# Strassen groups in a fused attention and MLP kernel: the first product of a group copied into the PSUM bank of the second

## The chip, the cores and the metric

The kernel runs on one NeuronCore of a Trainium2 chip. The metric is the device time of one execution in microseconds (us); less is better. Where several executions were timed, the median is given.

## The reference

Inputs are q, k and v of shape (8, 8, 576, 64): batch, heads, sequence, head dimension. A linear attention is followed by a layer norm and a two-layer MLP with a residual:

```python
q_s = softmax(q, axis=-1)             # over the 64 of the head
k_s = softmax(k, axis=2)              # over the sequence
kv  = einsum('bhsd,bhse->bhde', k_s, v)  # 64 x 64 for each head
x   = (q_s @ kv) as (8, 576, 512)     # heads side by side
xn  = (x - mean(x)) / sqrt(var(x) + 1e-6) * g_ln
out = x + relu(xn @ w_ch1) @ w_ch2    # 512 -> 2048 -> 512
```

All inputs and the output are float32; the kernel multiplies in 16 bit types. The first matrix product of the MLP, xn @ w_ch1 with its relu, is the part that the change touches.

## The kernel before

**Tiling.** The 8 x 576 tokens are cut into nine chunks of 512: chunks 0 to 7 hold the first 512 tokens of each batch entry (transposed tokens in `xsT`), and chunk 8 (`xT8`) holds the last 64 tokens of all eight. For each chunk the first MLP product gives `hT`, 16 row blocks of 128 hidden units by 512 tokens in float16, and the second (`mm2_split`, line 735) multiplies that with w_ch2. `attn(b + 1)` for the next batch entry (queries, keys, values, the products kv, xT and xT_last) runs beside the MLP of entry b.

**Order of the work.** No engine decides its order at run time. Each step is a task of the class `Plan` (line 100) with an engine, an assumed duration, what it reads and writes, and a class number. `Plan.order` plays the schedule through with these durations and an assumed 0.12 us from one engine to another; whenever an engine is free it takes the ready task with the lowest class. The instructions are then emitted in that order, and each engine works through its own list strictly. The table `SHIFT` (line 22) adds a number to the class of a task by its name and by the phase that it was made in: `early` for chunks 1 and 2, `steady` for 3 to 6, `last` for 7, `end` for 8. Tasks made for chunk 0, and the attention of batch entry 1, are made with no phase, and no entry of the table applies to them (line 137).

**The seven-product groups.** From chunk 3 on `mm1_seven` (line 882) makes the first MLP product. Most row blocks are made by `direct` (line 940): four matmuls of 128x512 into one of the four PSUM banks `pg`, and a relu on ScalarE (line 631). Some groups of four row blocks, the units n = 1 and n = 3, are made by a Strassen-Winograd scheme with seven products instead of eight. `UNITS` (line 841) says which: unit 1 in chunks 3 to 6, units 1 and 3 in chunks 7 and 8, eight units in all. A product is four matmuls of 128x256 (line 914). A unit holds three PSUM banks: `g[0]`, `g[1]` and `g[2]`, all three from the four banks `pa` that the attention products use too. It has three SBUF buffers `cp` for partial sums: the tiles `cp0` to `cp2`, which `add_x` and `final` of `mm2_split` use as well, or in chunks 7 and 8 the staging tiles `stg`.

The steps of a unit that the change and the prediction touch are:

- product "11" x "11" into bank `g[0]`, which stays open for further products
- `copy(0, 0)` (line 920): ScalarE copies this bank to the SBUF buffer 0
- product "12" x "21" into bank `g[1]`, as a group of its own
- `end(1, 0, 0, 0)` (lines 933 and 936): VectorE adds bank `g[1]` and buffer 0 into `hT`, then takes the maximum with 0 in place
- the rest: products "S2" x "T2" and "S3" x "T3" added to `g[0]`, two more copies (L920), further ends; a quarter of `hT` needs no partial sum and gets its relu on ScalarE directly (line 930)

**Other users of PSUM.** `mm2_split` takes three `pg` banks in turn for each chunk (gc, gb, ga, line 738) and holds ga from its first product to its last. Banks are given out in turn (`nxt`, line 297), in the order in which tasks are made, and not by which one is free.

**Loads.** SyncE's queue issues loads, transposes and stores. The loads of q, k and v land in `stg`, and ScalarE reads them from there: exponentials at lines 424 and 454, a cast at line 464.

Of the kernel before, what the change touches and what calls it, by code (L numbers as in the profile page):

```python
# [13 lines left out]
FP16 = mybir.dt.float16  # L14
BF16 = mybir.dt.bfloat16
U32 = mybir.dt.uint32
AF = mybir.ActivationFunctionType
# [2 lines left out]


SHIFT = {
    ('add_x1', 'early'): 0.6,
    ('add_x1', 'last'): -0.4,
    ('add_x1', 'steady'): 0.6,
    ('copy1', 'last'): 0.1,
    ('copy1', 'steady'): -0.1,
    ('direct1', 'last'): 1,
    ('dma_t1', 'early'): 0.2,
    ('dma_t1', 'steady'): -0.1,  # L30
    ('end1', 'end'): 0.4,
    ('end2', 'last'): -0.4,
    ('end2', 'steady'): 0.4,
    ('end3', 'end'): -0.6,
    ('end3', 'last'): -0.4,
    ('end3', 'steady'): 0.2,
    ('end4', 'end'): 0.1,
    ('final1', 'early'): -1,
    ('final1', 'end'): -0.1,
    ('final1', 'last'): 0.1,  # L40
    ('final2', 'end'): -0.6,
    ('final3', 'early'): 1,
    ('final3', 'end'): 1,
    ('final3', 'last'): 0.2,
    ('final3', 'steady'): 0.2,
    ('keys1', 'steady'): -0.4,
    ('kv1', 'early'): -0.4,
    ('kv1', 'steady'): -1,
    ('kv2', 'early'): 0.1,
    ('kv2', 'steady'): 0.6,  # L50
    ('kv3', 'early'): 0.4,
    ('kv4', 'early'): 0.1,
    ('load1', 'early'): 0.6,
    ('load1', 'steady'): -0.1,
    ('mm11', 'early'): -0.4,
    ('product1', 'end'): 0.1,
    ('product2', 'steady'): -1,
    ('queries1', 'early'): -0.4,
    ('queries1', 'steady'): -0.4,
    ('queries2', 'early'): -0.2,  # L60
    ('queries2', 'steady'): 0.2,
    ('queries3', 'early'): -1,
    ('queries3', 'steady'): -0.2,
    ('queries4', 'early'): -1,
    ('relu_evac1', 'early'): 0.4,
    ('relu_evac1', 'last'): 0.4,
    ('relu_evac1', 'steady'): -0.1,
    ('store2', 'early'): -0.1,
    ('store2', 'last'): 0.4,
    ('store2', 'steady'): 0.1,  # L70
    ('tokens3', 'early'): 0.2,
    ('tokens3', 'last'): 1,
    ('tokens6', 'last'): 0.1,
    ('tokens6', 'steady'): 0.6,
    ('tokens7', 'early'): 0.2,
    ('tokens7', 'last'): 0.4,
    ('tokens7', 'steady'): -0.6,
    ('tokens8', 'early'): -0.2,
    ('tokens8', 'last'): 0.2,
    ('tokens9', 'early'): -1,  # L80
    ('tokens9', 'steady'): 0.2,
    ('tt1', 'early'): 0.2,
    ('tt1', 'end'): -1,
    ('tt1', 'last'): 0.6,
    ('tt1', 'steady'): 1,
    ('tt3', 'early'): 1,
    ('tt3', 'steady'): -1,
    ('tt4', 'steady'): 0.6,
    ('values3', 'steady'): -0.1,
    ('xT1', 'early'): 1,  # L90
    ('xT1', 'steady'): -0.1,
    ('xT3', 'early'): -0.6,
    ('xT3', 'steady'): 0.2,
    ('xT_last1', 'steady'): 0.4,
    ('xT_last2', 'early'): 0.1,
    ('xT_last2', 'steady'): -0.4,
}


# [114 lines left out]
def act_t(n, extra=0.0):  # L214
    return 0.19 + 0.000833 * n + extra
# [7 lines left out]
def kernel(  # L223
# [10 lines left out]
    nc = tc.nc  # L234
    B, H, SEQ, D = q.shape
    DM = H * D
    DH = 4 * DM
    P = 128
# [14 lines left out]
    def sb(shape, dt, name):  # L253
        return persist.tile(shape, dt, name=name, tag=name)
# [42 lines left out]
    def nxt(what, n):  # L297
        i = cnt[what] % n
        cnt[what] += 1
        return i  # L300
# [23 lines left out]
    def sk(s):  # L324
        return [("stg", s, 0), ("stg", s, 1)]
# [268 lines left out]
    def tokens(c, cls=1, after=(), stats=()):  # L594

        x, xk, sti, stk = xof(c)
        if c < B:
            src, r = xsT[c % 2], XK(c % 2)
        else:
            src, r = xT8, [("xT8", b, i) for b in range(B) for i in range(2)]  # L600
        i = None
        for hf in range(2) if c == 0 else ():
            t = nxt("pa", 4)
            v = pa[t].bitcast(FP16)
            def f(hf=hf, v=v):
                for n in range(8):
                    nc.tensor.transpose(v[:, n * P : n * P + P], src[:, 8 * hf + n, :], ident_h)
            plan.task("tokens1", "PE", 0.52, f, r=r + ["ident_h"], w=[("pa", t)], cls=0, after=after)
            plan.task("tokens2", "DVE", dve_t(1024, 2), lambda hf=hf, v=v: nc.vector.tensor_copy(
                x[:, 2 * hf : 2 * hf + 2, :], v.rearrange("p (j n) -> p j n", j=2)), r=[("pa", t)], w=[(xk, 2 * hf), (xk, 2 * hf + 1)], cls=cls)  # L610
        if c:
            i = plan.task("tokens3", "SP", 2.2, lambda: nc.sync.dma_start_transpose(x.rearrange("p j (k c) -> p (j k) c", k=KO1), src.rearrange("p n t -> p (n t)")),
                     r=r, w=[(xk, j) for j in range(J)], mb=0.9, land=0.6, after=after)
        for j in STATS_ACT.get(c, ()):
            plan.task("tokens4", "ACT", act_t(512, 0.1), lambda j=j: nc.scalar.activation(junk, x[:, j, :], AF.Copy, saturate=False, scale=-(DM ** -1.5), accum_out=bmv[:, j, 0:1]),
                     r=[(xk, j)], w=[("bmv", j), "junk"], cls=SCLS, slack=2.0, after=stats)
            plan.task("tokens5", "ACT", act_t(512, 0.1), lambda j=j: nc.scalar.activation(junk, x[:, j, :], AF.Square, saturate=False, bias=bmv[:, j, 0:1], scale=DM ** -0.5, accum_out=bmv[:, j, 1:2]),
                     r=[(xk, j)], w=[("bmv", j), "junk"], cls=SCLS)
        for j in set(range(J)) - set(STATS_ACT.get(c, ())):
            plan.task("tokens6", "DVE", dve_t(512), lambda j=j: nc.vector.bn_stats(bst[:, j, :], x[:, j, :]), r=[(xk, j)], w=[("bst", j)], cls=cls, slack=2.0 if c else 0.0, after=stats)  # L620
            plan.task("tokens7", "DVE", 0.18, lambda j=j: nc.vector.bn_aggr(bmv[:, j, :], bst[:, j, :]), r=[("bst", j)], w=[("bmv", j)], cls=cls)
        plan.task("tokens8", "ACT", 0.3, lambda: nc.scalar.activation(sti[:, 3, :], bmv[:, :, 1], AF.Ln, bias=eps, scale=GS * GS),
                 r=["eps"] + [("bmv", j) for j in range(J)], w=[(stk, "v", j) for j in range(J)], cls=0)
        state["rstd"] = plan.task("tokens9", "ACT", 0.2, lambda: nc.scalar.activation(sti[:, 4, :], sti[:, 3, :], AF.Exp, scale=-0.5),
                                 r=[(stk, "v", j) for j in range(J)], w=[(stk, "r", j) for j in range(J)], cls=0)
        return i
# [215 lines left out]
    UNITS = {3: (1,), 4: (1,), 5: (1,), 6: (1,), 7: (1, 3), 8: (1, 3)}  # L842
    SUMS_AT = {2: (1,), 6: (3,)}
    flat = lambda t, n: t.bitcast(FP16).rearrange("p a j c -> p (a j c)")[:, :n].rearrange("p (i k n) -> p i k n", i=n // 512, k=2)
    WS = [flat(eq[n // 2], 1536) if n % 2 == 0 else sb([P, 3, 2, 256], FP16, f"WS{n}") for n in range(4)]
    WSK = [[("eq", n // 2, 0), ("eq", n // 2, 1)] if n % 2 == 0 else [] for n in range(4)]
    SLOT = (0, 1, None, 2)

    def w1_sums(n, before):
# [32 lines left out]
    def mm1_seven(c):  # L882
# [14 lines left out]
        class Unit:  # L897
            def __init__(self, n):
                self.n = n
                if last:  # L900
                    a = 3 * (n % 2)
                    self.g = [bufs[a + i] for i in range(3)] if n ^ 1 in units else [(pa[i], ("pa", i)) for i in [nxt("pa", 4) for _ in range(3)]]
                    self.cp = [(stg[a + i][:, :512], sk(a + i)) for i in range(3)]
                else:
                    self.g = [(pa[i], ("pa", i)) for i in [nxt("pa", 4) for _ in range(3)]]
                    self.cp = [(cp[i], [("cp", i)]) for i in range(3)]

            def product(self, a, b, g, first, last):
                fa, (fb, kb) = A[a], Bm[b]
                bank, bk = self.g[g]  # L910
                def f():
                    for i in range(2):
                        for k in range(2):
                            nc.tensor.matmul(bank[:, 256 * i : 256 * i + 256], fa(self.n, k, i), fb(k),  # L914
                                             start=(first and i == 0 and k == 0), stop=(last and k == 1), skip_group_check=True)
                ids.append(plan.task("product2", "PE", 0.437, f, r=kb + ([("WS", self.n, int(a[1]) - 1)] if a[0] == "S" else []), w=[bk]))

            def copy(self, g, n):
                bank, bk = self.g[g]
# [29 lines left out]
        for n0 in (0, 2):  # L949
            us = [Unit(n) for n in (n0, n0 + 1) if n in units]  # L950
            for u in us:
                u.product("11", "11", 0, True, False)
                u.copy(0, 0)
                u.product("12", "21", 1, True, True)
                u.end(1, 0, 0, 0)
            for u in us:
                u.product("S2", "T2", 0, False, False)
                u.copy(0, 1)
# [111 lines left out]
```

## Time and profile before

| what | value |
|---|---|
| median of six runs | 274.26 us (273.57 to 274.64) |
| the profiled execution's own time | 274.23 us |
| its span, first to last instruction | 272.4 us |
| PE busy | 264.0 us, 97% of the span |
| VectorE (DVE) busy | 228.1 us, 84% |
| ScalarE (ACT) busy | 170.0 us, 62% |
| granted TensorE clock | 0.998 |

The span is the time between the first and the last instruction in the trace; 1.83 us of the profiled execution's 274.23 us lie outside it. PE is TensorE. A matmul's row in the profile lasts longer than the time until the next one can start: a 128x256 matmul shows 273 ns, yet four of them in a row take 0.44 us. So PE busy is a union of overlapping rows, and progress on PE is read from the starts.

### The profile page before, as it was taken

The page shows a single profiled execution, that of the slowest core. Times are in us where ns is not written, and L with a number is a line of the kernel's source. Part 1 is how long each engine was busy: PE and PEld are TensorE (multiplying, and loading weights), DVE is VectorE, ACT ScalarE, POOL GpSimd, SP SyncE. Part 2 cuts the span into 40 slices and gives each one's busy share as a digit, 9 for nine tenths or more (in the row PEclk, how much of TensorE's full clock was granted, in tenths as well). Part 3 has the DMA queues.
Part 4 walks back from the last instruction along what each step waited for, and adds up shares of the span by engine and source line. Part 5 has one row for each costly group of instructions (what it writes and reads, how often), then busy time and mean ns, then how long its engine had stood idle before and what let it go on. Part 6 is the DMA issues. An engine that isn't in the chain of part 4 may idle for free.

```text
span 272.4 us, 5957 instructions
## 1 busy us (share of the span) xinstructions
PE 264.0 (97%) x2415; PEld 172.4 (63%) x2415; DVE 228.1 (84%) x484; ACT 170.0 (62%) x282; POOL 1.7 (1%) x12
## 2 busy tenths in 40 slices
PE   8799999999999999999999999999999999999994
PEld 3333445346864488548865786578558886786683
DVE  2897998898969889988998899989998897875772
ACT  4777866689598596578546955676562268325500
POOL 2000000000000000000000000000000000000000
PEclk9999999999999999999999999999999999999999
DMA  7999999699979999899288945995650960005004
GB/s 262 363 386 388 388 388 236 187 314 269 327 259 169 200 391 127 151 312 322 57 147 247 370 80 106 232 378 126 155 88 2 141 170 1 2 0 147 10 2 154
DMA packets 55875, 54.85 MB, mean 201 GB/s; under 512 B 34596, under 2 KB 35112, under 8 KB 55848
## 3 DMA queue, kind: packets, MB, share of 16 engines
q1 hardware_dynamic: 55696, 54.34, 71.7%
q8 instruction: 19, 0.31, 0.5%
q10 hardware_dynamic: 152, 0.13, 0.1%
q14 instruction: 8, 0.07, 0.1%
HBM read 36.70 MB, written 9.44 MB: 169 GB/s over the span
## 4 chain that ended last, share of the span: by engine, by line
PE 84%; DMA 9%; ACT 2%; SPq 1%; DVE 1%; issue 1%; ACTq 0%
PE pg L748 31%; PE pg L945 20%; PE pg L668 11%; PE pa L914 9%; DMA stg<-in_moe_w_ch_dram 7%; PE pg L812 5%; DMA stg<-in_k_dram 2%; PE pa L475 2%; PE pa L506 1%; PE pa L668 1%; PE pa L748 1%; SPq L321 1%; ACT ek L454 1%; PE pa L529 0%; PE pg L372 0%
## 5 line engine op out<-in xcount | busy, mean ns | idle before, releaser
L631 ACT ACTIVATE hT<-pg 128x512 f16<-128x512 f32 x102 | 60.2, 596 | 37.9 <-PE pg L945 28.4
L748 PEld LDWEIGHTS <-S 128*128 128x128 f16 x512 | 49.6, 98 | 7.1 <-DVE ot L759 0.4
L945 PE MATMUL pg<-xsT,w_sb 128*128 128x512 f16 x224 | 52.9, 379 | 0.0
L748 PE MATMUL pg<-T,S 128*128 128x256 f16 x368 | 43.6, 273 | 0.0
L748 PEld LDWEIGHTS <-hT 128*128 128x128 f16 x384 | 37.2, 98 | 7.4 <-issue 1.6
L945 PEld LDWEIGHTS <-w_sb 128*128 128x128 f16 x256 | 24.8, 98 | 23.2
L668 PE MATMUL pg<-xsT,w_sb 128*128 128x512 f16 x168 | 37.6, 379 | 0.7 <-DVE w_sb L378 0.7
L668 PEld LDWEIGHTS <-w_sb 128*128 128x128 f16 x184 | 17.4, 97 | 22.4 <-DVE w_sb L378 1.5
L684 DVE TENSOR_TENSOR S<-hT 128x1024 f16<-128x1024 f16 x32 | 21.6, 683 | 9.9 <-ACT hT L631 8.1
L748 PE MATMUL pg<-w_sb,hT 128*128 128x256 f16 x248 | 29.2, 273 | 0.0
L759 DVE SCALAR_TENSOR_TENSOR ot<-pg,st,cp 128x256 f32<-128x256 f32 x47 | 20.5, 477 | 6.6 <-PE pg L748 6.5
L426 DVE TENSOR_REDUCE zq<-eq 128x18 f32<-128x1152 bf16 x16 | 21.5, 1344 | 4.6 <-ACT eq L424 4.6
L759 DVE SCALAR_TENSOR_TENSOR cp<-pg,st,x 128x256 f32<-128x256 f32 x46 | 20.2, 478 | 5.8 <-PE pg L748 5.4
L620 DVE BATCH_NORM_STATS2 bst<-x 128x6 f32<-128x512 f16 x36 | 23.7, 675 | 0.0
L424 ACT ACTIVATE eq<-stg 128x1152 bf16<-128x1152 f32 x16 | 18.5, 1163 | 7.6 <-DMA stg<-in_q_dram 7.6
L430 DVE TENSOR_TENSOR eq<-eq,rzq 128x1152 bf16<-128x1152 bf16 x16 | 21.7, 1357 | 0.5
L519 ACT CAST xsT<-pa 128x512 f16<-128x512 f32 x31 | 16.0, 595 | 6.8 <-PE pa L506 6.8
L454 ACT ACTIVATE ek<-stg 128x1152 bf16<-128x1152 f32 x16 | 18.6, 1166 | 2.5 <-DMA stg<-in_k_dram 2.5
L464 ACT CAST vb<-stg 128x1152 f16<-128x1152 f32 x15 | 17.1, 1166 | 1.9 <-DMA stg<-in_v_dram 1.8
L748 PE MATMUL pg<-w_sb,S 128*128 128x256 f16 x128 | 15.6, 273 | 0.0
L914 PEld LDWEIGHTS <-w_sb 128*128 128x128 f16 x128 | 12.4, 98 | 4.7
L812 PE MATMUL pg<-w_sb,hT 128*128 128x512 f16 x64 | 14.7, 380 | 0.0
(100 smaller groups left out, 292.7 us busy)
## 6 DMA issues: line engine op xcount, KB each, us to landing
stg<-in_q_dram SPq DMA_DIRECT2D x16, 576.0 KB, 5.7
stg<-in_k_dram SPq DMA_DIRECT2D x16, 576.0 KB, 7.4
stg<-in_v_dram SPq DMA_DIRECT2D x16, 576.0 KB, 8.9
out_dram<-ot SPq DMA_DIRECT2D x33, 256.0 KB, 4.4
stg<-in_moe_w_ch_dram SPq DMA_DIRECT2D x16, 512.0 KB, 10.5
out_dram<-ot SPq DMA_DIRECT2D x1, 512.0 KB, 2.8
out_dram<-ot SPq DMA_DIRECT2D x1, 128.0 KB, 2.7
out_dram<-ot ACTq DMA_DIRECT2D x1, 128.0 KB, 2.2
```

What stands on the lines that cost most here:

```text
L426: plan.task("queries2", "DVE", dve_t(QW), lambda: nc.vector.reduce_sum(zq[:, hf], eh, axis=AX.X), r=[("eq", u, hf)], w=[("zq", hf)], cls=q ...
L430: plan.task("queries4", "DVE", dve_t(QW), lambda: nc.vector.tensor_tensor(eh, eh, rzq[:, hf].to_broadcast([P, 2 * JT, D]), op=ALU.mult), r ...
L454: plan.task("keys1", "ACT", act_t(QW), lambda: nc.scalar.activation(ek[u][:, hf].rearrange("p j (s d) -> p s j d", s=2), sv(s), AF.Exp), r ...
L620: plan.task("tokens6", "DVE", dve_t(512), lambda j=j: nc.vector.bn_stats(bst[:, j, :], x[:, j, :]), r=[(xk, j)], w=[("bst", j)], cls=cls, ...
L631: nc.scalar.activation(hT[:, m, :], bank, AF.Relu)
L668: nc.tensor.matmul(bank[gi], w1_sb[:, ko, m * P : m * P + P], xt[:, ko], start=(ko == 0), stop=(ko == KO1 - 1))
L684: plan.task("tt1", "DVE", dve_t(256 * n, 2), lambda: nc.vector.tensor_tensor(S[i][:, ks], a, b, op=op), r=r, w=sk(i), cls=(-0.25 if i < 2 ...
L748: nc.tensor.matmul(g[i][0], fa(k, i), fb(k), start=(first and k == 0 and (i == 0 or g[0][1] != g[1][1])), stop=(last and k == HK - 1), ski ...
L759: nc.vector.scalar_tensor_tensor(dst[:, i, :], in0=g[i][0], scalar=sti[:, 4, 2 * t0 + i : 2 * t0 + i + 1], in1=src[:, i, :], op0=ALU.mult, ...
L812: nc.tensor.matmul(pg[gis[j]], hT[:, kk, j * P : j * P + P], w2_sb[:, kk, :], start=(kk == 0), stop=(kk == KO2 - 1))
L914: nc.tensor.matmul(bank[:, 256 * i : 256 * i + 256], fa(self.n, k, i), fb(k), start=(first and i == 0 and k == 0), stop=(last and k == 1), ...
L945: nc.tensor.matmul(bank, w1_sb[:, ko, m * P : m * P + P], xt[:, ko], start=(ko == 0), stop=(ko == KO1 - 1))
```

## The change

Five things are edited.

1. A new method `seed` copies bank `g[0]` with ScalarE into bank `g[1]`, in place of the copy into SBUF. The product "12" x "21" is then made without a start flag, so that it adds to what the copy wrote. The end of this quarter becomes the ScalarE relu of line 930; the VectorE add and maximum are dropped for it.
2. Bank `g[1]` of every unit comes from `pg` and no longer from `pa`. The cases for chunks 7 and 8 are written as one rule with the others.
3. `WS[0]` and `WS[2]`, weight sums for the units 0 and 2, are placed in other tiles. `UNITS` has only units 1 and 3, so neither is written or read.
4. The assumed durations of `tokens4` and `tokens5` are changed. `STATS_ACT` is empty, so no such task is made.
5. The table `SHIFT` is replaced by another one with some 80 entries, among them three for `seed1`.

```diff
 SHIFT = {
-    ('kv2', 'early'): 0.1,
-    ('kv3', 'early'): 0.4,
-    ('load1', 'early'): 0.6,
+    ('keys1', 'early'): 1,
+    ('kv2', 'early'): -1,
+    ('kv3', 'early'): 0.2,
+    ('load1', 'early'): 0.2,
+    ('seed1', 'end'): 0.6,
+    ('seed1', 'last'): -1,
+    ('seed1', 'steady'): -0.1,
...
 class Unit:
     def __init__(self, n):
         self.n = n
-        if last:
-            a = 3 * (n % 2)
-            self.g = [bufs[a + i] for i in range(3)] if n ^ 1 in units else [(pa[i], ("pa", i)) for i in [nxt("pa", 4) for _ in range(3)]]
-            self.cp = [(stg[a + i][:, :512], sk(a + i)) for i in range(3)]
-        else:
-            self.g = [(pa[i], ("pa", i)) for i in [nxt("pa", 4) for _ in range(3)]]
-            self.cp = [(cp[i], [("cp", i)]) for i in range(3)]
+        new = lambda name, ts: (lambda i: (ts[i], (name, i)))(nxt(name, 4))
+        self.g = [new("pa", pa), new("pg", pg), new("pa", pa)]
+        a = 3 * (n % 2)
+        self.cp = [(stg[a + i][:, :512], sk(a + i)) if last else (cp[i], [("cp", i)]) for i in range(3)]
...
+    def seed(self, g, d):
+
+        (bank, bk), (to, tk_) = self.g[g], self.g[d]
+        plan.task("seed1", "ACT", act_t(512), lambda: nc.scalar.copy(to, bank), r=[bk], w=[tk_], cls=-0.3)
...
     for u in us:
         u.product("11", "11", 0, True, False)
-        u.copy(0, 0)
-        u.product("12", "21", 1, True, True)
-        u.end(1, 0, 0, 0)
+        u.seed(0, 1)
+        u.product("12", "21", 1, False, True)
+        u.end(1, 0, 0)
```

More of the change, by code (lines that the diff above doesn't have):

```diff
@@ L22 @@
 SHIFT = {
-    ('add_x1', 'early'): 0.6,
-    ('add_x1', 'last'): -0.4,
+    ('add_x1', 'early'): -0.1,
+    ('add_x1', 'end'): 0.1,
+    ('add_x1', 'last'): 1,
     ('add_x1', 'steady'): 0.6,
[L26 to L42, printed above, removed]
+    ('copy1', 'end'): 0.6,
+    ('copy1', 'last'): -0.1,
+    ('copy1', 'steady'): 0.1,
+    ('direct1', 'end'): -0.1,
+    ('direct1', 'last'): -1,
+    ('direct1', 'steady'): 0.1,
+    ('dma_t1', 'steady'): 0.1,
+    ('end1', 'end'): 0.2,
+    ('end1', 'last'): -0.2,
+    ('end1', 'steady'): 0.2,
+    ('end2', 'end'): 0.4,
@@ L43 @@
+    ('end2', 'last'): 0.6,
+    ('end2', 'steady'): 0.2,
+    ('end3', 'steady'): -0.2,
+    ('end4', 'end'): -0.1,
+    ('final1', 'early'): 0.6,
+    ('final1', 'end'): 0.4,
+    ('final1', 'last'): -0.2,
+    ('final2', 'end'): -0.2,
+    ('final3', 'early'): 0.4,
     ('final3', 'end'): 1,
-    ('final3', 'last'): 0.2,
+    ('final3', 'last'): -0.4,
     ('final3', 'steady'): 0.2,
-    ('keys1', 'steady'): -0.4,
+    ('final4', 'end'): -0.4,
+    ('keys1', 'early'): 1,
+    ('keys1', 'steady'): 0.1,
@@ L47 @@
     ('kv1', 'early'): -0.4,
-    ('kv1', 'steady'): -1,
-    ('kv2', 'early'): 0.1,
-    ('kv2', 'steady'): 0.6,
-    ('kv3', 'early'): 0.4,
-    ('kv4', 'early'): 0.1,
-    ('load1', 'early'): 0.6,
[L54 to L62, printed above, removed]
-    ('queries3', 'steady'): -0.2,
@@ L64 @@
[L64 to L73, printed above, removed]
-    ('tokens6', 'steady'): 0.6,
[L75 to L79, printed above, removed]
@@ L80 @@
-    ('tokens9', 'early'): -1,
-    ('tokens9', 'steady'): 0.2,
+    ('kv2', 'early'): -1,
+    ('kv2', 'steady'): 0.4,
+    ('kv3', 'early'): 0.2,
+    ('kv4', 'early'): -0.4,
+    ('kv4', 'steady'): 0.2,
+    ('load1', 'early'): 0.2,
+    ('mm11', 'early'): 0.4,
+    ('product1', 'end'): 0.4,
+    ('product1', 'last'): -0.6,
+    ('product1', 'steady'): -0.6,
+    ('product2', 'end'): -0.1,
+    ('product2', 'last'): -0.1,
+    ('queries1', 'steady'): 0.2,
+    ('queries2', 'early'): 1,
+    ('queries2', 'steady'): 0.1,
@@ new lines @@
+    ('queries3', 'early'): -0.6,
+    ('queries3', 'steady'): -0.2,
+    ('queries4', 'steady'): -0.6,
+    ('relu_evac1', 'early'): 0.1,
+    ('relu_evac1', 'end'): 0.6,
+    ('relu_evac1', 'steady'): -1,
+    ('seed1', 'end'): 0.6,
+    ('seed1', 'last'): -1,
+    ('seed1', 'steady'): -0.1,
+    ('store1', 'end'): 0.6,
+    ('store2', 'early'): 1,
+    ('store2', 'last'): -0.4,
+    ('store2', 'steady'): -1,
+    ('tokens3', 'early'): 0.1,
+    ('tokens3', 'last'): -0.1,
+    ('tokens3', 'steady'): -0.1,
@@ L82 @@
+    ('tokens6', 'early'): 0.1,
+    ('tokens6', 'last'): 1,
+    ('tokens6', 'steady'): 0.6,
+    ('tokens8', 'early'): -1,
+    ('tokens8', 'last'): -0.2,
+    ('tokens9', 'early'): 0.6,
+    ('tokens9', 'last'): 0.4,
+    ('tokens9', 'steady'): 1,
     ('tt1', 'early'): 0.2,
-    ('tt1', 'end'): -1,
-    ('tt1', 'last'): 0.6,
-    ('tt1', 'steady'): 1,
+    ('tt1', 'end'): 0.6,
+    ('tt1', 'last'): 0.4,
+    ('tt1', 'steady'): -0.4,
     ('tt3', 'early'): 1,
-    ('tt3', 'steady'): -1,
-    ('tt4', 'steady'): 0.6,
@@ L89 @@
[L89 to L96, printed above, removed]
+    ('tt3', 'steady'): -0.6,
+    ('tt4', 'last'): 0.1,
+    ('tt4', 'steady'): -0.1,
+    ('values3', 'steady'): 1,
+    ('xT1', 'early'): -0.2,
+    ('xT3', 'early'): 0.1,
+    ('xT_last2', 'early'): -0.4,
+    ('xT_last2', 'steady'): 0.4,
 }
@@ L614, in tokens @@
         for j in STATS_ACT.get(c, ()):
-            plan.task("tokens4", "ACT", act_t(512, 0.1), lambda j=j: nc.scalar.activation(junk, x[:, j, :], AF.Copy, saturate=False, scale=-(DM ** -1.5), accum_out=bmv[:, j, 0:1]),
+            plan.task("tokens4", "ACT", act_t(512, 0.23), lambda j=j: nc.scalar.activation(junk, x[:, j, :], AF.Copy, saturate=False, scale=-(DM ** -1.5), accum_out=bmv[:, j, 0:1]),
                      r=[(xk, j)], w=[("bmv", j), "junk"], cls=SCLS, slack=2.0, after=stats)
-            plan.task("tokens5", "ACT", act_t(512, 0.1), lambda j=j: nc.scalar.activation(junk, x[:, j, :], AF.Square, saturate=False, bias=bmv[:, j, 0:1], scale=DM ** -0.5, accum_out=bmv[:, j, 1:2]),
+            plan.task("tokens5", "ACT", act_t(512, 0.32), lambda j=j: nc.scalar.activation(junk, x[:, j, :], AF.Square, saturate=False, bias=bmv[:, j, 0:1], scale=DM ** -0.5, accum_out=bmv[:, j, 1:2]),
                      r=[(xk, j)], w=[("bmv", j), "junk"], cls=SCLS)
@@ L844 @@
     flat = lambda t, n: t.bitcast(FP16).rearrange("p a j c -> p (a j c)")[:, :n].rearrange("p (i k n) -> p i k n", i=n // 512, k=2)
-    WS = [flat(eq[n // 2], 1536) if n % 2 == 0 else sb([P, 3, 2, 256], FP16, f"WS{n}") for n in range(4)]
-    WSK = [[("eq", n // 2, 0), ("eq", n // 2, 1)] if n % 2 == 0 else [] for n in range(4)]
+    WS = [ek[0], None, eq[0], None]
+    WS = [sb([P, 3, 2, 256], FP16, f"WS{n}") if n % 2 else flat(WS[n], 1536) for n in range(4)]
+    WSK = [[("ek", 0, 0), ("ek", 0, 1)], [], [("eq", 0, 0), ("eq", 0, 1)], []]
     SLOT = (0, 1, None, 2)
```

## Prediction, made before the changed kernel was run

> **What bounds the kernel now.** I read the page's table of engines first:
>
> ```profile
> PE 264.0 (97%) x2415; PEld 172.4 (63%) x2415; DVE 228.1 (84%) x484; ACT 170.0 (62%) x282; POOL 1.7 (1%) x12
> ```
>
> PE is busy for 97% of the span. Since a matmul's row outlasts its share of PE, this alone proves little, so the second view is the busy time in stretches of 10 us (columns: PE, PEld, DVE, ACT, POOL, clock, DMA share, GB/s):
>
> ```profile
> 30.00:40.00 10.00, 10.00 (x48) 4.54 (x47) 9.51 (x14) 7.31 (x9) 0.00 (x0) 1.00 1.05 387
> ...
> 70.00:80.00 10.00, 9.57 (x155) 7.57 (x156) 7.02 (x20) 7.07 (x11) 0.00 (x0) 1.00 0.92 343
> ...
> 110.00:120.00 10.00, 10.00 (x122) 5.27 (x120) 9.33 (x25) 5.75 (x12) 0.00 (x0) 1.00 0.98 220
> ...
> 220.00:230.00 10.00, 10.00 (x79) 7.48 (x77) 8.02 (x19) 8.81 (x18) 0.00 (x0) 1.00 0.27 70
> ```
>
> From 30 to 260 us PE has 10.00 in every stretch except 70 to 80. The rates agree: the chain of work in order of time gives 3.49 us for 32 matmuls of 128x256 and 0.86 us for four of 128x512, 109 and 216 ns each, back to back. Third, PE's own waits and the end of the chain:
>
> ```profile
> PE pa L506 <- ACT kve L489: 0.4, 1, 0.4
> ```
>
> ```profile
> 27.63 7.08 PE pg L668 x32
> ...
> 267.66 0.89 PE pa L748 x8
> 268.55 0.03 issue
> 268.57 0.48 DVE ot L759
> ```
>
> The one wait of PE after 27.6 us is 0.43 us near 76.3 us, behind kve on ScalarE. So 27.6 us are a start limited by weight loads, 241 us are PE without gaps but for that one, and 3.8 us (272.4 - 268.6) are the last VectorE step and store. Nothing in the start has a phase, so the new order table can't reach it; the tail is the same code.
>
> [...] The trace has no ScalarE write to PSUM. [...] at 76.33 kve sat behind an exponential of the next entry that had waited 0.34 us for its load, and PE stood.
>
> **The change part by part.** The rows, by shape:
>
> ```profile
> L933 DVE TENSOR_TENSOR hT<-pa,cp 128x512 f16<-128x512 f32 x12 | 8.2, 683 | 0.9 <-PE pa L914 0.9
> L920 ACT COPY cp<-pa 128x512 f32<-128x512 f32 x12 | 6.9, 586 | 6.5 <-DVE ot L759 4.9 <-PE pa L914 1.6
> L930 ACT ACTIVATE hT<-pa 128x512 f16<-128x512 f32 x8 | 4.8, 596 | 0.1
> L936 DVE TENSOR_SCALAR hT<-hT 128x512 f16<-128x512 f16 x16 | 4.7, 293 | 0.5
> ```
>
> Removed from VectorE: eight adds at 0.683 us (one of L933's three in each of eight units) and eight maxima at 0.293: 7.8 us of 228.1. Added on ScalarE: eight relus at 0.596, 4.8 us. Eight copies change their target: nearest row 0.586; [...] I take 0.586. ScalarE goes from 170 to about 175. Neither engine is the bound: its effect on the time is 0 while PE is fed, and a gain is excluded wherever PE is at 10.00, since freed VectorE time can only feed an engine that is not hungry.
>
> On PE: the same 2415 matmuls in the same shapes. A start flag costs nothing that the rows show (273 ns with and without). So the work term is 0.
>
> What moves is a wait. Now "12" x "21" follows the first product at once:
>
> ```profile
> 98.40 1.05 PE L914 MATMUL pa<-xsT,w_sb 128*128 128x256 f16 x8
> ...
> 101.56 1.16 ACT L454 ACTIVATE ek<-stg 128x1152 bf16<-128x1152 f32 x1 [0.33 <-DMA stg<-in_k_dram]
> ...
> 102.63 0.57 ACT L920 COPY cp<-pa 128x512 f32<-128x512 f32 x1
> ...
> 104.09 0.60 PE L914 MATMUL pa<-x,WS 128*128 128x256 f16 x4
> ```
>
> The x8 is both products. Afterwards the second must wait for the seed, behind it on PE stands everything emitted later, and behind PE both other engines. The round trip: in chunk 7 the first product starts at 216.13, its four matmuls take PE 0.44, and the copy starts at 216.77, so 0.20 after PE is free for the next; then 0.59 for the copy; then about 0.05 to PE (kve ended at about 76.63, L506 went at 76.68). Together 0.84 us. The planner assumed 0.12 + 0.617 + 0.12 = 0.86, so a plan without a gap should run without a gap, as it does now for "S2" x "T2", which already waits for such a copy. Cover: one direct block (0.86) or two products (0.87) emitted in between, and each chunk has 12 or 8 direct blocks, and the seven products of the second MLP matrix product, to choose from. Without any cover the cost is 8 x 0.84 = 6.7 us; with it 0. I take 0.
>
> Bank g[1] leaves `pa` for `pg`. The unit then uses the one `pg` bank that mm2_split's three leave over; `pa` is relieved. Cost between 0 and the displaced direct blocks (below). I take 0. The buffer cp0 no longer serves the units, so ScalarE's waits there (L920 for VectorE, 4.9 us in 4) shrink; PE doesn't stand behind them, so 0.
>
> The WS placement and the tokens4 and tokens5 durations make no instruction: 0. The new table shifts orders on all queues, SyncE's loads included. It can remove the 0.43 us at 76 us (kv and key classes of phase early change) or keep it; I keep it, as the late load is what caused it.
>
> Sum, against the profiled execution: 274.23 + 0 (PE work) + 0 (seed waits covered) + 0 (banks) + 0 (stall kept) = 274.2. That execution is 0.03 from the median of 274.26, so the forecast needs no correction.
>
> **The rivals.** *The late seed (slower).* ScalarE's list holds exponentials and casts that wait for loads, and a seed emitted behind one is late by what the load is late:
>
> ```profile
> ACT eq L424 <- DMA stg<-in_q_dram: 7.6, 7, 3.0
> ...
> ACT ek L454 <- DMA stg<-in_k_dram: 2.5, 7, 0.5
> ...
> ACT vb L464 <- DMA stg<-in_v_dram: 1.8, 4, 0.6
> ```
>
> That is 18 waits of 0.66 us on average (11.9 / 18), 3.0 at most. The four steady units lie among such loads; chunks 7 and 8 come after the last such load. Today the copy after such a load delays only "S2" x "T2", which has more work ahead of it. If two or three of the four seeds are hit by 0.66 each beyond their cover, the loss is 1.3 to 2.0 us, 1.7 in the middle: 275.9. It decides once the delays beyond the cover sum to over 0.82 us. For it: the load wait just ahead of the copy at 101.56. Against it: this copy would still have come 0.9 us ahead of its product at 104.09.
>
> *The bank (slower).* In chunk 4 three direct blocks stand among the second MLP product (at 131.1, 135.5 and 138.1) as cover while VectorE works; each takes a `pg` bank. If the unit's bank displaces them and PE has nothing else ready, up to three blocks of 0.86 are bare: 2.6 us, 276.8. Against it: VectorE, which they wait for, has 7.8 us less to do.
>
> *The gap closes (faster).* The reordered loads and kve take the 0.43 us away: 274.23 - 0.43 = 273.8. This is still within 0.3%; more would need a shorter start or tail, for which I see no means. [...]
>
> **The chances.** Forecast as it stands 0.40, gap closes 0.15, late seed 0.33, bank 0.12. A difference under about 0.3% (0.82 us: 273.4 to 275.1) can't be told from none here. Faster by more: a part of the gap case and of the spread of single runs (273.57 at the lowest), 0.09. Slower by more: nearly all of the two slower cases, 0.40. Within: 0.51. The range runs from 273.5 (gap case with a little spread) to 276.8 (the bank case); the likeliest case alone has 273.8 to 274.7.
>
> **What would show it.** Right: the stretches from 80 to 260 us have 10.00 on PE; VectorE's busy time is near 220.3 and ScalarE's near 175; L930 appears 16 times, the copies to `cp` and `stg` 16 in all. Wrong: PE waits for ScalarE's seed in the list of waits (late seed), or for relus at L631 or VectorE at L759 releasing `pg` banks (bank), or a start or tail of other length than 27.6 and 3.8 us.

## The result and the profile after

The changed kernel takes 276.88 us in the median of 17 runs (275.02 to 277.98), the kernel before 274.37 us in 36 runs beside it: ratio 1.0084, 95% interval 1.0066 to 1.0101. It is slower by 0.84% (0.91% by the two medians alone), just above the upper edge of the predicted range, where no change was forecast. The 17 times lie in two groups: eight at 275.0 to 275.8 with a granted clock of 0.998 to 1.000, nine at 276.9 to 278.0 with 0.993 or 0.994. Their medians are 275.49 and 277.74. The profiled execution took 277.97 (span 276.1), so it shows the upper group.

Line numbers have moved: L914 is now L921, L748 is L757, L506 (xT) is L515, L519 (its casts) is L528, L529 (xT_last) is L538, L424 and L454 (exponentials of q and k) are L433 and L463. In the kernel before, `mm2_split` begins at line 721 and takes its banks at 724, and `UNITS` stands at 842. The engines of the changed kernel first:

```profile
PE 266.4 (96%) x2415; PEld 173.5 (63%) x2415; DVE 222.1 (80%) x468; ACT 173.2 (63%) x290; POOL 1.7 (1%) x12
```

The work moved the way that was predicted, by somewhat less: the same 2415 matmuls, VectorE 6.0 us less (7.8 were forecast), ScalarE 3.2 us more (4.8). The stretches of 10 us then show a hole that was not there before (columns as in the prediction; PE, PEld, DVE, ACT, POOL, clock):

```profile
70.00:80.00 10.00, 10.00 (x164) 7.97 (x162) 7.30 (x22) 5.33 (x11) 0.00 (x0) 1.00 1.00 311
...
100.00:110.00 10.00, 7.70 (x60) 6.02 (x59) 4.30 (x11) 6.70 (x10) 0.00 (x0) 0.83 0.67 170
110.00:120.00 10.00, 10.00 (x70) 6.66 (x69) 9.72 (x16) 5.61 (x10) 0.00 (x0) 1.00 0.41 105
```

The old gap at 76 us is closed. PE stands 2.3 us between 100 and 110, and the clock there is 0.83. Cut finer, the loss of clock is one stretch of 3.4 us at half speed, after the standstill:

```profile
105.50:108.90 3.40, 3.40 (x18) 2.43 (x17) 1.10 (x3) 2.53 (x5) 0.00 (x0) 0.50 0.74 116
```

PE calls this stretch fully busy. Only the clock column, and 18 matmuls where about 31 fit (3.4 / 0.109), tell that half of it is lost. PE's list of waits names the releaser:

```profile
PE pa L538 <- ACT xsT L528: 2.3, 2, 2.0
```

No seed is in that list. The timeline of the changed kernel around the place, and then that of the kernel before:

```profile
91.63 1.16 ACT L463 ACTIVATE ek<-stg 128x1152 bf16<-128x1152 f32 x1
...
94.00 0.83 PE L484 MATMUL pa<-vb,ek 64*64 64x65 f16 x72
...
96.01 1.16 ACT L433 ACTIVATE eq<-stg 128x1152 bf16<-128x1152 f32 x1 [1.15 <-DMA stg<-in_q_dram]
...
97.92 0.63 PE L515 MATMUL pa<-eqT,kve 64*64 64x512 bf16 x8
98.09 1.16 ACT L433 ACTIVATE eq<-stg 128x1152 bf16<-128x1152 f32 x1 [0.92 <-DMA stg<-in_q_dram]
...
100.98 1.16 ACT L463 ACTIVATE ek<-stg 128x1152 bf16<-128x1152 f32 x1 [1.73 <-DMA stg<-in_k_dram]
...
102.49 1.16 ACT L463 ACTIVATE ek<-stg 128x1152 bf16<-128x1152 f32 x1 [0.34 <-DMA stg<-in_k_dram]
103.56 2.03 ACT L528 CAST xsT<-pa 128x512 f16<-128x512 f32 x4
104.18 0.22 PE L538 MATMUL pa<-eqT,kve 64*64 64x64 bf16 x2 [2.03 <-ACT xsT L528]
```

```profile
89.75 0.83 PE L475 MATMUL pa<-vb,ek 64*64 64x65 f16 x72
...
94.93 0.63 PE L506 MATMUL pa<-eqT,kve 64*64 64x512 bf16 x8
...
95.59 2.05 ACT L519 CAST xsT<-pa 128x512 f16<-128x512 f32 x4
...
97.97 2.20 ACT L424 ACTIVATE eq<-stg 128x1152 bf16<-128x1152 f32 x2
98.21 0.26 PE L529 MATMUL pa<-eqT,kve 64*64 64x64 bf16 x8
```

Before, ScalarE cast the results of xT of entry 3 at once, and then turned to the exponentials of entry 4. After, the four exponentials of entry 4 stand first in its list and wait for their loads, 4.1 us in all. The casts, whose input was there at 98.5 (97.92 + 0.63), start at 103.56. They free the `pa` banks that xT_last writes, so PE stands, with the whole second MLP product behind it. All this happens before the first seed of the kernel runs, at 110.7.

The account of the profiled execution, from matmul start to matmul start: the steady part begins at 27.95 and no longer at 27.63 (+0.32); the standstill takes 2.62 (2.20 before xT_last and 0.42 inside it); 17 matmuls at 213 ns in place of 109 lose 1.77; the gap at 76 us, with the slack around it, is gone (-0.76). That is +3.95 against a measured 277.97 - 274.23 = 3.74; the last 0.2 us are spread over the rest.

### The profile page after: what moved, and what is told of

Read it like the earlier page. It is cut to its first block, busy times and chain, and to the rows that moved or that the text cites. A ratio compares the mean times of both kernels' runs of the same rounds, so it can differ in the third digit from the quotient of the medians.

```text
span 276.1 us, 5943 instructions
## 1 busy us (share of the span) xinstructions
PE 266.4 (96%) x2415; PEld 173.5 (63%) x2415; DVE 222.1 (80%) x468; ACT 173.2 (63%) x290; POOL 1.7 (1%) x12
## 4 chain that ended last, share of the span: by engine, by line
PE 84%; DMA 10%; ACT 1%; SPq 1%; issue 1%; DVE 1%; ACTq 0%
PE pg L757 33%; PE pg L957 20%; PE pg L677 10%; PE pa L921 8%; DMA stg<-in_moe_w_ch_dram 7%; PE pg L821 5%; DMA stg<-in_k_dram 3%; PE pa L484 2%; PE pa L677 1%; PE pa L757 1%; PE pg L921 1%; PE pa L515 1%; SPq L330 1%; PE pa L538 0%; PE pg L381 0%
## 5 line engine op out<-in xcount | busy, mean ns | idle before, releaser
L757 PEld LDWEIGHTS <-S 128*128 128x128 f16 x512 | 50.4, 100 | 8.5 <-issue 0.8
L757 PE MATMUL pg<-T,S 128*128 128x256 f16 x368 | 46.4, 278 | 0.0
L757 PEld LDWEIGHTS <-hT 128*128 128x128 f16 x384 | 37.1, 98 | 9.4 <-issue 1.6
L757 PE MATMUL pg<-w_sb,hT 128*128 128x256 f16 x248 | 30.7, 273 | 0.0
L433 ACT ACTIVATE eq<-stg 128x1152 bf16<-128x1152 f32 x16 | 18.3, 1163 | 6.2 <-DMA stg<-in_q_dram 6.2
L463 ACT ACTIVATE ek<-stg 128x1152 bf16<-128x1152 f32 x16 | 18.6, 1169 | 4.4 <-DMA stg<-in_k_dram 4.4
L528 ACT CAST xsT<-pa 128x512 f16<-128x512 f32 x31 | 16.1, 593 | 4.6 <-PE pa L515 4.6
L757 PE MATMUL pg<-w_sb,S 128*128 128x256 f16 x128 | 15.7, 275 | 0.0
L921 PEld LDWEIGHTS <-w_sb 128*128 128x128 f16 x128 | 12.4, 98 | 4.0
L757 PE MATMUL pg<-T,hT 128*128 128x256 f16 x120 | 14.7, 273 | 0.0
```

Of the source, the lines that this page charges most:

```text
L433: plan.task("queries1", "ACT", act_t(QW), lambda: nc.scalar.activation(e.rearrange("p j (s d) -> p s j d", s=2), sv(s), AF.Exp), r=sk(s), ...
L463: plan.task("keys1", "ACT", act_t(QW), lambda: nc.scalar.activation(ek[u][:, hf].rearrange("p j (s d) -> p s j d", s=2), sv(s), AF.Exp), r ...
L757: nc.tensor.matmul(g[i][0], fa(k, i), fb(k), start=(first and k == 0 and (i == 0 or g[0][1] != g[1][1])), stop=(last and k == HK - 1), ski ...
```

## The experiments

The theory: the new order table puts exponentials that wait for loads ahead of the casts, and the rest follows. The rival: the seed, its wait, or its bank costs the time. Each kernel ran beside the kernel before.

### The casts first

```diff
             plan.task("queries1", "ACT", ...
-                ... slack=late, after=exps)
+                ... slack=late, after=tuple(exps) + (tuple(state["ev"][-1][-1:]) if b == 4 else ()))
...
             plan.task("keys1", "ACT", ...
-                ... slack=late, after=exps)
+                ... slack=late, after=tuple(exps) + (tuple(state["ev"][-1][-1:]) if b == 4 else ()))
```

> The changed kernel, with one more rule for the order: the exponentials of entry 4's queries and keys stand behind the four xsT casts of entry 3 in ScalarE's list. Theory (order and late loads): the new table lets four exponentials that wait for loads stand ahead of those casts, the casts free the pa banks that xT_last needs, and PE stands 2.6 us and then runs at half clock for a while. Without that order the stall goes: 273.9 us (273.5 to 274.4), in one cluster, PE without a wait after 28 us. Rival (the seed or its bank costs the time): nothing of that is touched, so 276.9 us in two clusters, as the changed kernel.

Measured: 273.61 us (14 runs, 273.18 to 275.11), ratio 0.9986 (0.9972 to 1.0000). The stall is gone: the casts come at 98.31 and xT_last at 101.14 without a wait.

```profile
98.31 2.05 ACT L528 CAST xsT<-pa 128x512 f16<-128x512 f32 x4 [3.51 <-PE pa L515]
100.49 1.17 ACT L463 ACTIVATE ek<-stg 128x1152 bf16<-128x1152 f32 x1
101.14 0.26 PE L538 MATMUL pa<-eqT,kve 64*64 64x64 bf16 x8
```

Seeds and banks are untouched, so the rival falls. The planner orders all tasks anew for such a rule, but played through with its assumed durations the new lists differ from those of the changed kernel in no more than 20 places for each of ScalarE, PE and VectorE, all between 95 and 121 us, and nowhere for SyncE. One part of the expectation missed: three of the 14 runs are at 274.8 to 275.1, at full clock, and the profile, of an execution of 273.56 us, doesn't show why.

### Entry 4's loads halved

```diff
+        n = 1 if b == 4 else 2
-        load(stg[s].rearrange("p (h r) -> p h r", h=2),
+        load(stg[s].rearrange("p (h r) -> p h r", h=2)[:, :n],
...
-             [:, 2 * hf : 2 * hf + 2],
+             [:, 2 * hf : 2 * hf + n],
```

> The changed kernel with every instruction in the same order, but the six loads of q, k and v of batch entry 4 bring half of their bytes (one of two heads; the other half of the staging tile keeps old values, so entry 4 is computed from partly wrong data). Theory (the loads land later than the planner assumed): they land some 2 to 3 us earlier, the casts are no longer held up, 274.0 us (273.6 to 274.6) in one cluster. Rival (the order alone is too tight, whatever the loads do): the stall of PE at xT_last stays above 1.5 us, 276 us or more.

Measured: 273.51 us (14 runs, 273.15 to 273.81), ratio 0.9971 (0.9961 to 0.9982), and xT_last is not in PE's list of waits. The last of the four exponentials starts at 98.04 in place of 102.49, more than the 2 to 3 us expected, and the casts follow at 99.11. The instructions stand in the faulty order, and it costs nothing when the loads come sooner. So it takes both: the order and the late loads.

### PE kept busy while it would stand

```diff
+            idle = pg[(cnt["pg"] + 3) % 4]
             def f():
+                for _ in range(8 if b == 3 else 0):
+                    nc.tensor.matmul(idle, w1_sb[:, 0, :P], w1_sb[:, 0, :512], start=True, stop=True, skip_group_check=True)
```

> The changed kernel, with eight matmuls of 128x512 into an idle pg bank ahead of entry 3's xT_last, so that PE works while it would stand there; they take 8 x 0.216 = 1.73 us of a stall of about 2.6 us. Theory (the upper of the two clusters of times comes from PE running at half clock after the stall): the upper cluster goes, all runs at 275.0 to 275.8, granted clock 1.00. Rival (the two clusters come from loads that land at two different times): both clusters stay, 275.0 to 275.8 and 276.9 to 278.0, and if PE's added work doesn't fit, later still.

Measured: 275.44 us (5 runs, 275.10 to 275.63), ratio 1.0044 (1.0032 to 1.0057), clock 0.999 or 1.000 in each. The row of the same stretch:

```profile
100.00:110.00 10.00, 9.75 (x88) 7.70 (x86) 6.44 (x14) 7.28 (x11) 0.00 (x0) 1.00 0.66 165
```

The time lost to the stall remains and the upper group is gone. With more work on PE the kernel is 1.4 us quicker than the changed kernel's median. In this profile the loads also came sooner than in that of the changed kernel (the casts start at 102.68, not 103.56), so five runs of this kernel alone don't rule out that the loads made a part of the difference. The same is tried on a longer stall in "The fault alone, with PE kept busy".

### The seed without cover

```diff
         seq = self.order()
+        for first, seed, second in self.units:
+            seq.remove(first)
+            seq.remove(second)
+            i = seq.index(seed)
+            seq[i : i + 1] = [first, seed, second]
```

> The changed kernel, with each unit's first product, its seed and its second product moved next to each other in the emitted order, so that nothing stands on PE between the first and the second product. It prices the wait that the prediction called covered. Theory: 0.84 us for each of eight units, 6.7 us on top of the changed kernel's 275.4 or 276.9: 282 to 284 us, and PE's list of waits shows the seed eight times with about 0.8 us. Rival (the wait is cheaper, since the second product's weights load and ScalarE starts early): under 0.4 us each, 280 us or less.

Measured: 283.31 us (6 runs, 282.82 to 285.26), ratio 1.0327 (1.0312 to 1.0341). Five of the six ran at a clock of 0.998 or more, to be held against 275.49: 7.8 us for eight seeds. In this kernel L927 is a product of a unit, L934 the seed and L544 xT_last:

```profile
PE pg L927 <- ACT pg L934: 5.9, 8, 1.1
PE pa L544 <- ACT xsT L534: 1.9, 2, 1.7
```

The list counts 5.9 us, since a matmul's row (272 ns) outlasts its share of PE (109 ns). From start to start the seven plain cases lose 0.82 to 0.88 us each and one 1.23, 7.2 in sum; where the other 0.6 us lie is not shown. The round trip of 0.84 was priced rightly, and in the changed kernel it is covered eight times out of eight.

The sixth run is the profiled one, of 285.26 us at a clock of 0.992. Its half rate follows the standstill at xT_last and not a seed: the first seed's gap begins at 110.69, and the clock from 110 to 120 us is 1.00.

```profile
100.00:110.00 10.00, 7.96 (x61) 6.10 (x60) 4.65 (x12) 6.70 (x10) 0.00 (x0) 0.83 0.68 172
110.00:120.00 10.00, 9.29 (x65) 6.27 (x65) 8.95 (x15) 5.12 (x9) 0.00 (x0) 1.00 0.41 105
```

### The fault alone, in the kernel before

```diff
         seq = self.order()
+        i = seq.index(self.casts[12])
+        for e in [e for e in seq[i:] if e in self.exps]:
+            seq.remove(e)
+            seq.insert(i, e)
+            i += 1
```

Here `casts` collects the xsT casts and `exps` the four exponentials of entry 4 as they are made.

> The kernel before (no seed, its own table and banks), with one thing moved: the four exponentials of entry 4 stand ahead of the four xsT casts of entry 3 in ScalarE's list, as in the changed kernel. Theory (this order with late loads is the whole loss): in the kernel before the last of those exponentials ended at 102.7 us and xT_last went at 98.2; with the casts behind it xT_last goes at about 103.4, so PE stands some 5 us, and half a stretch at half clock may follow: 279 to 282 us, with xT_last waiting for xsT at the head of PE's waits. Rival (the order hurts only together with the seed or the new banks): 274.3, no change.

Measured: 281.61 us (6 runs, 280.64 to 283.86), ratio 1.0271 (1.0229 to 1.0312). PE's waits and the stretch:

```profile
PE pa L538 <- ACT xsT L527: 4.9, 2, 4.7
```

```profile
100.00:110.00 10.00, 6.83 (x41) 4.87 (x41) 3.86 (x7) 5.88 (x11) 0.00 (x0) 0.66 0.54 155
```

With no seed, no new bank and no new table the same stall comes, longer, since xT stood earlier here. The clock was 0.991 in three runs and 0.987 in the other three.

### The fault alone, with PE kept busy

The kernel just above, and 20 matmuls into an idle bank as in the third experiment.

> The kernel before with the planted order of the exponentials, which took 281.6 us in six runs at a granted clock of 0.991 or 0.987, and 20 matmuls of 128x512 (4.3 us) into an idle pg bank ahead of entry 3's xT_last. Theory (after a long stall PE runs at half clock for a while, and that is part of the loss): the stall's own length stays, about 5.3 us, but the clock stays at 1.00 and the loss shrinks by 1.7 to 3 us: 279.0 to 280.2 in one cluster. Rival (the clock has nothing to do with it, and the spread comes from the loads): 281.6 again, 280.6 to 283.9.

Measured: 280.26 us (5 runs, 279.58 to 281.17), ratio 1.0216 (1.0189 to 1.0243). Four runs have a clock of 0.998 or more and one 0.994.

```profile
100.00:110.00 10.00, 9.59 (x82) 7.19 (x81) 6.66 (x13) 6.52 (x13) 0.00 (x0) 1.00 0.71 155
```

The clock stays up, where all six runs without the added matmuls had 0.987 or 0.991. The medians differ by 1.35 us, less than the 1.7 to 3 expected, and the intervals of the two ratios overlap, so the size of the gain is open. Nor are the times in a single group; the profile shows a further gap of 0.7 us at entry 6's xT_last, which the other profiles don't have.

### The seed undone, with the new table

```diff
-                u.seed(0, 1)
-                u.product("12", "21", 1, False, True)
-                u.end(1, 0, 0)
+                u.copy(0, 0)
+                u.product("12", "21", 1, True, True)
+                u.end(1, 0, 0, 0)
```

> The changed kernel with its table and its banks, but the old steps of a unit put back: copy into SBUF buffer 0, second product as a group of its own, add and maximum on VectorE. Rival (the seed and its wait cost the time): undoing it gives the time back, 274.5 us or less. Theory (the seed costs nothing, it relieves VectorE, and the table was made for it): no gain, the stall at entry 3's xT_last stays, and the units' extra VectorE work and the buffer shared with add_x open new gaps: 278 us or more.

Measured: 276.85 us (4 runs, 276.31 to 277.80), ratio 1.0092 (1.0071 to 1.0113). The rival's gain doesn't come, but the 278 of the theory was too high (L757 is a product of `mm2_split`):

```profile
PE pa L538 <- ACT xsT L528: 1.5, 2, 1.2
...
PE pg L757 <- DVE cp L768: 0.8, 2, 0.5
```

The stall is there, 1.8 us from start to start in the profiled run, and the clock stayed at 0.997 to 1.000 in all four runs. New waits for VectorE's use of `cp`, 0.8 us in the list, come in addition. Since two things differ, this run can't price the seed. The next one can.

### The seed undone, with the stall out of the way

The same edit and, as in the last experiment below, entry 4's loads assumed later.

> The changed kernel with the seed undone (copy to SBUF, add and maximum on VectorE; new table, new banks) and with entry 4's loads assumed later, so that the stall at xT_last is out of the comparison. Against the same kernel with the seed (273.5 us) it gives what the seed itself is worth. Theory (the seed relieves VectorE, for which PE waits in three places of 0.3 to 0.7 us when it is undone): 274.5 to 275.5. Rival (the seed costs its round trip somewhere): below 273.4.

Measured: 274.30 us (14 runs, 273.89 to 275.67), ratio 0.9997 (0.9979 to 1.0016), against 273.54 with the seed. So the seed is worth about 0.8 us to this table, and 274.30 is a little under the 274.5 to 275.5 that was expected. The intervals of the two ratios just touch, at 0.9979, so the size is rough. The new waits are VectorE's:

```profile
PE pg L757 <- DVE cp L768: 0.6, 1, 0.6
```

### The seed with the old table

The changed kernel with the `SHIFT` of the kernel before.

> The changed kernel (seed, new banks) with the order table of the kernel before. It asks whether the structure could have been had without the new table. Theory: the casts of entry 3 stand ahead of the exponentials again, so no stall at that place, but a table made for another list of tasks leaves gaps of its own, of several us in sum, from chunk 3 on: 280 us or more, PE waiting in several places. Rival (the new table is the only fault, the old one would do): 273.6 to 274.5.

Measured: 284.66 us (4 runs, 284.49 to 285.50), ratio 1.0379 (1.0361 to 1.0398).

```profile
PE pa L912 <- DVE x L876: 4.7, 2, 4.1
PE pg L748 <- DVE S L684: 1.8, 2, 1.5
```

Lines are numbered here as in the kernel before (L912 is a product of a unit, L748 one of `mm2_split`, L876 and L684 are sums that VectorE makes for them). There is no stall at xT_last, but there are others of up to 4.3 us from chunk 4 on, and the longest comes with 6.8 us at half rate. The old table doesn't fit the new list of tasks; that each list needs a table of its own is more than one run shows.

### The loads assumed later

```diff
-        late = 1.5 if steady else 0.0
+        late = (5.0 if b == 4 else 1.5) if steady else 0.0
```

> The changed kernel, with the planner told that entry 4's loads can be used 5.0 us after it thinks that they land, in place of 1.5. The order then has two exponentials of queries, the four casts of entry 3, and the two exponentials of keys only later. Theory (the assumed landing time made the wrong order): no stall of PE at xT_last, 273.6 us (273.2 to 274.2). Rival (two late exponentials ahead of the casts are enough): a stall of 0.5 us or more at xT_last, 274.5 to 275.5.

Measured: 273.54 us (6 runs, 273.24 to 273.71), ratio 0.9966 (0.9953 to 0.9979): quicker than both kernels. After 28 us PE waits for nothing. As with the casts first, the planner's lists differ from those of the changed kernel only near this place.

## Why the prediction was wrong

**Right.** PE's work didn't change, and the bound was PE. The round trip of a seed (0.84, measured 0.82 to 0.88) and its cover were right. The bank moved at no visible cost (with the loads assumed later PE waits for nothing after 28 us); whether it could have stayed in `pa` no run shows. The start and the tail kept their lengths (27.95, of which two transfers of the weights take 8.44 and 10.81 in the chain, where the starts in the other traces end at 27.5 to 28.2, and 276.1 - 272.3 = 3.8 us). The relus and copies came out as counted:

```profile
L942 ACT ACTIVATE hT<-pg 128x512 f16<-128x512 f32 x8 | 4.8, 601 | 7.8 <-PE pg L921 7.7
L942 ACT ACTIVATE hT<-pa 128x512 f16<-128x512 f32 x8 | 4.8, 599 | 0.4 <-PE pa L921 0.4
...
L928 ACT COPY pg<-pa 128x512 f32<-128x512 f32 x8 | 4.6, 577 | 6.2 <-PE pa L921 6.1
```

The copy into PSUM takes 577 ns against 586 into SBUF: 9 ns are saved, and the 0.586 that the prediction took was near.

**The step that failed** is the one on the order table: "It can remove the 0.43 us at 76 us [...] or keep it". I looked for what a new order can do at the one gap that existed, and gave it no cost where there was none: the term stands in the sum as 0. It did close that gap: with the stall taken out the kernel runs at 273.54, near the 273.8 of the gap case. (From start to start the gap was 0.76 us, not the 0.43 of the list.) And it opened another at entry 3's xT_last: 2.62 us of standstill and 1.77 us of half clock in the profiled run, 1.95 us in all in the median of the lower group. A table is an edit of every queue, and its cost can't be bounded by the waits of the kernel before. What the profile did offer were the 18 waits of ScalarE for loads and the fact that the casts of xT release PE's banks; what stood behind those exponentials was the question to ask, not for the seeds alone.

**A sentence that was too strong** is "a plan without a gap should run without a gap". It follows from durations and round trips that fit, and loads don't fit: the chain of the changed kernel has the last k load of entry 4 as 9.16 us from issue to landing. Played through with the planner's assumed durations, the two exponentials of k start at 97.7 and 98.9; on the chip they started at 100.98 and 102.49. In the planner's own schedule the casts follow at 100.0 and nothing stands. Why the new table lets xT come at 97.92 rather than 94.93 is argued, not shown: the keys and values of entry 3 are spread among the relus of chunk 2, and kv goes 4.3 us later.

**The rivals.** The late seed had the mechanism, ScalarE in order behind a late load, and the wrong victim. Its 275.9 would have come from the four seeds; no seed made PE wait. The bank case had no part in it. Its 276.8 is near the median by accident.

**A term that was missing** is the clock. The stall on PE cost more than its length: another 1.77 us in the profiled run, and nine of the 17 runs have its clock. Here a standstill of 2.6 us was followed by 3.41 us at a clock of 0.50. Measured from start to start, other traces show half rate with standstills of 2.3 us (no cover, at xT_last), 4.3 us (old table) and 5.3 us (the fault alone), and none with 1.8 us (seed undone) and 1.7 us (old table, at 134). It lasts 3.41 us after the two shorter ones; with the two longer ones it begins before PE goes on, and lasts 6.83 us. The sum closes: 273.54 for the mended kernel, 275.49 with the stall (1.95), 277.74 with half clock (1.77) and, it seems, a stall longer by 0.5. So the runs that kept their clock seem to be those with the shorter stall; there is no profile of them, and whether the length alone decides is not shown.

**Open** are the three runs at 275 of the casts-first kernel, and what makes the same loads land earlier in one run than in another.

## What to carry to other kernels

Where each engine runs a fixed list, look in that list for what stands behind an instruction that waits for a DMA, and for whom that later work releases a buffer. A plan that assumes a landing time is as safe as that time is, and planning with a later one cost nothing here: 3.5 us more for one batch entry turned a loss of 0.8% into a gain of 0.3%. When an edit brings a new order along, count the order as a part of the change, with a price on both sides, even where the kernel before has no gap.

## What the runs showed of the hardware that was not expected

- A standstill of PE of 2.6 us was followed by 3.4 us at a clock of 0.50 (the changed kernel), and one of 2.3 us as well (no cover); standstills of 1.8 us (seed undone) and 1.7 us (old table) and eight gaps of 0.82 to 1.23 us (no cover, five of six runs at 0.998 or more) were not. PE's busy share reads 100% in such a stretch (3.40 us of 3.40).
- Matmuls that do nothing of use, put where PE would stand, kept the mean clock at 0.998 or more in nine of ten runs (0.994 in the tenth). After a stall of 5.3 us it had been 0.987 or 0.991 without them.
- A seed by ScalarE into a PSUM bank adds 0.82 to 0.88 us (1.23 in one case of eight) between the end of one product and the start of the next when nothing covers it.
